# An adaptive-layernorm attention block: a narrower first part of the scale, and four accumulators copied out early

## The chip, the cores and the metric

The kernel runs on one core of a Trainium2 chip. The core has a matrix engine (TensorE, "PE" in the profile), a vector engine (VectorE, "DVE"), an activation engine (ScalarE, "ACT"), GpSimd ("POOL"), and a queue engine (SyncE, "SP") that issues most transfers from HBM. Each engine runs its own instructions in order and waits on semaphores for the others. The metric is device time in microseconds (us) of one execution; lower is better.

## The reference

The inputs are x [2, 256, 1152], a conditioning vector c [2, 1152], and the bf16 weights wqkv [1152, 3456], wo [1152, 1152] and w_mod [1152, 6912].

```python
mod = (silu(c) @ w_mod).reshape(B, 6, 1, D)
shift_a, scale_a, gate_a, ... = [mod[:, i] for i in range(6)]
h = layernorm(x) * (1 + scale_a) + shift_a
q, k, v = split(h @ wqkv, 3)
p = softmax((q @ k.T) * D ** -0.5)
out = x + gate_a * ((p @ v) @ wo)
```

Only the first three sixths of w_mod matter: shift, scale and gate.

## The kernel before

D = 1152 is nine blocks of 128 (`KT`), and the 512 tokens are four tiles of 128 (`TT`), two to a batch. Everything up to the scores is kept transposed: the channel lies on the partitions, the token on the free axis.

**The problem at the start.** h needs scale and shift, each a product of silu(c) with 1152 x 1152 weights, and the projections need h. To have TensorE at work before the shift's weights (`wH`) have come, the kernel uses that h @ w = (xn * (1 + scale)) @ w + shift @ w. `xnT` is the transposed normalized x; `hTs` = `xnT` times (1 + scale), without the shift. The first seven column blocks of q (`NB` = 7, their weights are `wA`) are accumulated from `hTs`: six in `accs[0..5]` (banks of the pool `psum`, 128 x 512 f32 each), the seventh in `acc_last` (`last_acc`). Their shift part is 63 narrow matmuls (`bias_mms`) into `bias_ps`, added when the accumulators are evacuated to `qkT` (`acc_evac`). The other eleven column blocks of q and k, and v, use the full `hT` = `xnT` * (1 + scale) + shift (`modulated`), once the shift is there.

**The scale comes in two column parts.** `KA` = 5: `scale_block(psSA, ...)` gives the scale of channel blocks 0 to 4 from the first 640 columns of `wS`, in nine steps of contraction (kk) of five matmuls each; `psSB` gives blocks 5 to 8 from the other 512. The ones matmul that opens `psSA` makes it 1 + scale. So the accumulation can run with blocks 0 to 4 while the rest of `wS` is on its way.

**The transposes.** `transposes(t, h, ...)` makes half h of tile t: blocks 0 to 4 or 5 to 8 (`HALF` follows `KA`), by TensorE into a bank `tp`; `xnT_copy` brings it to SBUF, on VectorE (`True`) or ScalarE (`False`). Tiles 0 and 1 (batch 0) come before the accumulation; tiles 3 and 2 between its steps.

**The accumulation.** `qkv_half(k, b)` is channel block k for the tokens of batch b: six matmuls of 256 columns, one for each accumulator. `qkv_step(k)` does both batches at once, six of 512. Before: half steps for blocks 0 to 4 of both batches, steps for blocks 5 to 8. `shift_block(kk)` is a step of the shift, nine matmuls from `wH` into `bankH`. After the ninth, VectorE copies the shift to `sh_bf` and `sh`.

**What sets the order.** `pin()` fixes the order of PE, DVE, ACT and SP as written in the source; all recorded operations therefore have line L76 in the profile, and are told apart by their tiles. The pool `psum` has six banks, `psum_pre` two. A transfer of SP waits for the landing of the one eight before it. The load order on SP is x, the first part of `wS` (five transfers), `wA` rows 0 to 4 (three), the rest of `wS` (two), `wA` rows 5 to 8 (two), `wH` (five), then the other wqkv columns (`wq_t`), the gate's weights and wo.

**After the shift** come 18 `modulated` pieces, each one channel block of one batch; every third on ScalarE, the others on VectorE. Before, both evacuations of accumulator 1 stand after the fifteenth piece. Then VectorE forms the gate (`gacc`, 18 operations), TensorE the eleven `ps` blocks, the scores, v, p @ v and the last product.

Of the kernel before, what the change touches and what calls it, by code (L numbers as in the profile page):

```python
# [10 lines left out]
F32 = mybir.dt.float32  # L11
# [5 lines left out]
def kernel(  # L17
# [10 lines left out]
    P = 128  # L28
    B, N, D = x.shape
    T = B * N  # L30
    KT = D // P
# [7 lines left out]
    NACC = 6  # L39
    NB = 7  # L40
    WA = NB * P
    KA = 5
    CA = KA * P
    NRS = 96
    NRH = 54
    KH = KA
    N_JUNK = 11

    x_f = x.rearrange("b n d -> (b n) d")
# [4 lines left out]
    const = ctx.enter_context(tc.tile_pool(name="const", bufs=1))  # L54
    wpool = ctx.enter_context(tc.tile_pool(name="wpool", bufs=1))
    act = ctx.enter_context(tc.tile_pool(name="act", bufs=1))
# [3 lines left out]
    psum_pre = ctx.enter_context(tc.tile_pool(name="psum_pre", bufs=2, space=PSUM))  # L60
# [22 lines left out]
    vec = _Rec(nc.vector, dve_seq)  # L83
    sca = _Rec(nc.scalar, act_seq)
    ten = _Rec(nc.tensor, pe_seq)

    def pin(seq):
# [11 lines left out]
        out=ident, in_=ident, compare_op=ALU.not_equal, fill=1.0, base=0,  # L99
# [49 lines left out]
    def load_mod(tile_, which, k0, k1, c0, c1):  # L149
        spq.dma_start(out=tile_[:, k0:k1, c0:c1], in_=wmod_v[:, k0:k1, which, c0:c1])  # L150

    def load_wA(k0, k1):
        spq.dma_start(out=wA[:, k0:k1, :], in_=wqkv_v[:, k0:k1, 0:WA])
# [4 lines left out]
    load_wA(1, 3)  # L158
    load_wA(3, KA)
    load_mod(wS, 1, 0, 5, CA, D)  # L160
    load_mod(wS, 1, 5, KT, CA, D)
    load_wA(KA, 7)
    load_wA(7, KT)
    for k0, k1 in ((0, 2), (2, 4), (4, 6), (6, 8), (8, 9)):
        load_mod(wH, 0, k0, k1, 0, D)

# [5 lines left out]
    def fillers(n):  # L172
# [10 lines left out]
        out=scT_f.rearrange("p k b -> p b k"),  # L183
# [7 lines left out]
    def sc_rhs(kk, n):  # L191
        return scT_rep[:, kk].rearrange("p r b -> p (r b)")[:, 0:n]
# [9 lines left out]
    def dve_stats(t, s):  # L202
        vec.bn_stats(out=stats[t][:, s, :], in_=x_sb[:, t, s * CW : (s + 1) * CW])
# [6 lines left out]
    def dve_norm(t):  # L210
        vec.scalar_tensor_tensor(
            out=nb[:, t : t + 1], in0=mv_all[:, t, 0:1], scalar=-1.0, in1=rstd[:, t : t + 1],
            op0=ALU.mult, op1=ALU.mult,
        )
        vec.tensor_scalar(
            out=xn[:, t, :], in0=x_sb[:, t, :], scalar1=rstd[:, t : t + 1], scalar2=nb[:, t : t + 1],
            op0=ALU.mult, op1=ALU.add,
        )
# [15 lines left out]
    def act_norm(t):  # L234
        sca.activation(out=xn[:, t, :], in_=x_sb[:, t, :], func=ACT.Identity,
                       bias=nb[:, t : t + 1], scale=rstd[:, t : t + 1])

    tps = {}
    HALF = ((0, KA), (KA, KT))

    def transposes(t, h, pool, tag):
        k0, k1 = HALF[h]
        tp = pool.tile([P, KH, P], BF16, tag=tag, name="tp")
        for k in range(k0, k1):
            ten.transpose(tp[:, k - k0, :], xn[:, t, k * P : (k + 1) * P], ident)
        tps[t, h] = tp

    def xnT_copy(t, h, on_dve):
        k0, k1 = HALF[h]
        dst, srct = xnT[:, k0:k1, t * P : (t + 1) * P], tps[t, h][:, : k1 - k0, :]  # L250
        if on_dve:
            vec.tensor_copy(out=dst, in_=srct)
        else:
            sca.copy(out=dst, in_=srct)


    s1p = const.tile([P, KT, B], F32)
# [3 lines left out]

    psSA = psum_pre.tile([P, KA, NRS], F32, tag="pre")
    ten.matmul(psSA.rearrange("p j r -> p (j r)"), lhsT=ones_bf[0:1, :],
# [3 lines left out]
    def scale_block(ps_, n, k0, k1, kk, ones=True):  # L267
        for j in range(k0, k1):
            ten.matmul(
                ps_[:, j - k0, :], lhsT=wS[:, kk, j * P : (j + 1) * P], rhs=sc_rhs(kk, n),  # L270
                start=(kk == 0 and j == k0 and not ones), stop=(kk == KT - 1), skip_group_check=True,
            )

    def scaled(k, b, scalar):
        sl = slice(b * N, (b + 1) * N)
        vec.tensor_scalar(out=hTs[:, k, sl], in0=xnT[:, k, sl], scalar1=scalar, scalar2=None, op0=ALU.mult)

    def qkv_half(k, b):
        sl = slice(b * N, (b + 1) * N)
        for f in range(NACC):  # L280
            ten.matmul(
                accs[f][:, sl], lhsT=wA[:, k, f * P : (f + 1) * P], rhs=hTs[:, k, sl],
                start=(k == 0 and b == 0), stop=False, skip_group_check=True,
            )

    def qkv_step(k):
        for f in range(NACC):
            ten.matmul(
                accs[f], lhsT=wA[:, k, f * P : (f + 1) * P], rhs=hTs[:, k, :],
                start=False, stop=(k == KT - 1), skip_group_check=True,  # L290
            )

    def last_acc(k0, k1):
        for k in range(k0, k1):
            ten.matmul(
                accs[NACC], lhsT=wA[:, k, NACC * P : NB * P], rhs=hTs[:, k, :],
                start=(k == 0), stop=(k == KT - 1),
            )

    def shift_block(kk):  # L300
        for j in range(KT):
            ten.matmul(
                psH[:, j, :], lhsT=wH[:, kk, j * P : (j + 1) * P], rhs=sc_rhs(kk, NRH),
                start=(kk == 0 and j == 0), stop=(kk == KT - 1), skip_group_check=True,
            )
# [17 lines left out]
    xnT_copy(1, 1, False)  # L323
    scale_block(psSA, NRS, 0, KA, 2)
    scale_block(psSA, NRS, 0, KA, 3)
    dve_stats(2, 1)
    transposes(0, 0, psum, "mm")
    transposes(0, 1, psum, "mm")
    xnT_copy(0, 0, True)
    dve_stats(2, 2)  # L330
    dve_aggr(2)
    act_norm(3)
    xnT_copy(0, 1, False)
    for kk in range(4, KT):
        scale_block(psSA, NRS, 0, KA, kk)
    transposes(3, 0, psum_pre, "pre")
    xnT_copy(3, 0, False)

    accs = []
    for f in range(NACC):  # L340
# [2 lines left out]

    scaled(0, 0, psSA[:, 0, 0:1])
    vec.tensor_copy(out=s1p[:, 0:KA, :], in_=psSA[:, :, 0:B])
    for k in range(1, 4):
        scaled(k, 0, s1p[:, k, 0:1])
    dve_norm(2)
    scaled(4, 0, s1p[:, 4, 0:1])
    qkv_half(0, 0)  # L350
    qkv_half(1, 0)
    qkv_half(2, 0)
    transposes(2, 0, psum_pre, "pre")
    xnT_copy(2, 0, True)
    qkv_half(3, 0)
    transposes(3, 1, psum_pre, "pre")
    xnT_copy(3, 1, False)
    qkv_half(4, 0)
    transposes(2, 1, psum_pre, "pre")
    xnT_copy(2, 1, False)  # L360
    for k in range(KA):
        scaled(k, 1, s1p[:, k, 1:2])
    for k in range(3):
        qkv_half(k, 1)
    psSB = psum_pre.tile([P, KT - KA, NRH], F32, tag="pre")
    for kk in range(KT):
        scale_block(psSB, NRH, KA, KT, kk, ones=False)
# [2 lines left out]
        for b in range(B):  # L370
            scaled(k, b, s1p[:, k, b : b + 1])
    qkv_half(3, 1)
    qkv_half(4, 1)


    bankH = psum_pre.tile([P, 512], F32, tag="pre")
    psH = bankH[:, 0 : KT * NRH].rearrange("p (k r) -> p k r", k=KT)
    bias_ps = bankH[:, KT * NRH : KT * NRH + NB * B].rearrange("p (f b) -> p f b", b=B)
    accs.append(psum_pre.tile([P, T], F32, tag="pre", name="acc_last"))
    qkv_step(5)  # L380
    qkv_step(6)
    shift_block(0)
    shift_block(1)
    qkv_step(7)
    for kk in range(2, 5):
        shift_block(kk)
    last_acc(0, 3)
    shift_block(5)
    shift_block(6)
    shift_block(7)  # L390
    qkv_step(8)
    acc0_sb = const.tile([P, T], F32)
    sca.copy(out=acc0_sb, in_=accs[0])
    last_acc(3, 6)
    shift_block(8)
    vec.tensor_copy(out=sh_bf, in_=psH[:, :, 0:B])
# [16 lines left out]
    def modulated(i):  # L413
        k, b = divmod(i, B)
        sl = slice(b * N, (b + 1) * N)
        if i % 3 == 2:
            sca.activation(
                out=hT[:, k, sl], in_=xnT[:, k, sl], func=ACT.Identity,
                bias=sh[:, k, b : b + 1], scale=s1p[:, k, b : b + 1],
            )  # L420
        else:
            vec.tensor_scalar(
                out=hT[:, k, sl], in0=xnT[:, k, sl],
                scalar1=s1p[:, k, b : b + 1], scalar2=sh[:, k, b : b + 1],
                op0=ALU.mult, op1=ALU.add,
            )
# [3 lines left out]
    def acc_evac(f, b, on_dve):  # L430
        sl = slice(b * N, (b + 1) * N)
        if on_dve:
            vec.tensor_scalar(
                out=qkT[:, f, sl], in0=accs[f][:, sl], scalar1=bias_sb[:, f, b : b + 1],
                scalar2=None, op0=ALU.add)
        else:
            sca.activation(
                out=qkT[:, f, sl], in_=accs[f][:, sl], func=ACT.Identity,
                bias=bias_sb[:, f, b : b + 1], scale=1.0)

    for i in range(15):
        modulated(i)
    vec.tensor_copy(out=bias_sb, in_=bias_ps)
    for b in range(B):
        acc_evac(1, b, True)
    for i in range(15, KT * B):
        modulated(i)
    accs[0] = acc0_sb
    for f, on_dve in ((2, False), (3, True), (4, False), (5, True), (6, False), (0, True)):
        for b in range(B):  # L450
            acc_evac(f, b, on_dve)

# [35 lines left out]
    for b in range(B):  # L488
        vec.tensor_scalar(
            out=gacc[:, b, :], in0=wg_k[0], scalar1=scT_f[:, 0, b : b + 1], scalar2=None, op0=ALU.mult  # L490
        )
        for kt in range(1, KT):
            vec.scalar_tensor_tensor(
                out=gacc[:, b, :], in0=wg_k[kt],
# [37 lines left out]
    for b in range(B):  # L532
# [7 lines left out]
        for i in range(NQ):  # L540
            sca.activation(
                out=p_f[:, i, :], in_=s_ps[:, i, :], func=ACT.Exp,
# [43 lines left out]
    for t in range(TT):  # L586
        b = t // NQ
# [67 lines left out]
```

## Time and profile before

| | |
|---|---|
| median of 3 runs | 103.08 us (102.88 to 103.28) |
| the profiled execution, time | 102.94 us |
| the profiled execution, span from first to last instruction | 101.2 us |
| mean granted TensorE clock | 0.994 |
| busy: PE, DVE, ACT, POOL | 94.1, 71.7, 30.9, 29.1 us |
| HBM read, written | 19.76 MB, 1.18 MB |

The span is what the profile's clock starts and ends with; the rest of the time (1.7 us) lies around it. "Busy" of PE counts matmuls whose ends are modelled, so it overstates how full the engine is; starts of matmuls are what can be compared. In a timeline line the numbers are start and length, then engine, line, operation, out<-in, engine array, shapes and count; the bracket at its end gives the idle time before it and what ended that. In the chain a line has start, length, and the engine or transfer. In a windows line the columns are the stretch and its length, then busy time and instruction count of PE, PEld, DVE, ACT and POOL, the granted clock, the share of the DMA engines, and GB/s.

### The profile page before, as it was taken

The page shows a single profiled execution, that of the slowest core. Times are in us where ns is not written, and L with a number is a line of the kernel's source. Part 1 is how long each engine was busy: PE and PEld are TensorE (multiplying, and loading weights), DVE is VectorE, ACT ScalarE, POOL GpSimd, SP SyncE. Part 2 cuts the span into 40 slices and gives each one's busy share as a digit, 9 for nine tenths or more (in the row PEclk, how much of TensorE's full clock was granted, in tenths as well). Part 3 has the DMA queues.
Part 4 walks back from the last instruction along what each step waited for, and adds up shares of the span by engine and source line. Part 5 has one row for each costly group of instructions (what it writes and reads, how often), then busy time and mean ns, then how long its engine had stood idle before and what let it go on. Part 6 is the DMA issues. An engine that isn't in the chain of part 4 may idle for free.

```text
span 101.2 us, 1878 instructions
## 1 busy us (share of the span) xinstructions
PE 94.1 (93%) x769; PEld 58.1 (57%) x773; DVE 71.7 (71%) x129; ACT 30.9 (31%) x61; POOL 29.1 (29%) x29
## 2 busy tenths in 40 slices
PE   1999899999999799999999999999998999999970
PEld 0228779956657244444447865656567765665650
DVE  1599754240029999999999999955626857989960
ACT  5378904000039932422422013146215500000000
POOL 5038300000000000000799100000898000999700
PEclk9999999999999999999999999999999999999997
DMA  2999999999999999999999700000000000303122
GB/s 38 371 319 343 392 357 367 384 391 385 349 369 342 373 383 333 302 323 327 331 379 389 284 13 0 0 0 0 6 0 3 0 0 0 117 6 117 69 80 85
DMA packets 16963, 21.06 MB, mean 208 GB/s; under 512 B 827, under 2 KB 12603, under 8 KB 16955
## 3 DMA queue, kind: packets, MB, share of 16 engines
q1 hardware_dynamic: 16523, 20.34, 59.6%
q10 hardware_dynamic: 432, 0.61, 2.2%
q8 instruction: 6, 0.10, 0.4%
q14 instruction: 2, 0.02, 0.1%
HBM read 19.76 MB, written 1.18 MB: 207 GB/s over the span
## 4 chain that ended last, share of the span: by engine, by line
PE 66%; DMA 18%; SPq 7%; DVE 5%; issue 1%; ACT 0%
PE ps L76 59%; DMA wH<-in_w_mod_dram 12%; SPq L76 7%; DMA wS<-in_w_mod_dram 7%; PE s_ps L76 4%; DVE hT L76 3%; PE acc_t L76 1%; DVE qkT L76 1%; PE bankH L76 1%; PE acc_last L76 1%; DVE pT L76 0%; PE pT_ps L76 0%; ACT o_sb L76 0%; DVE sh_bf L76 0%; DVE sh L76 0%
## 5 line engine op out<-in xcount | busy, mean ns | idle before, releaser
L497 POOL PARTITION_ALL_REDUCE gate_bc<-gacc x2 | 14.1, 7067 | 51.7 <-DVE gacc L76 36.5
L76 DVE SCALAR_TENSOR_TENSOR gacc<-wG,scT_f,gacc 128x1152 f32<-128x1152 bf16 x16 | 27.4, 1714 | 0.6
L76 PE MATMUL ps<-hT,wq_t 128*128 128x512 bf16 x97 | 21.6, 379 | 0.6 <-DVE hT L76 0.5
L76 PE MATMUL ps<-wq_t,hT 128*128 128x384 bf16 x108 | 17.7, 326 | 0.0
L76 PEld LDWEIGHTS <-wq_t 128*128 128x128 bf16 x99 | 9.5, 98 | 12.3 <-DVE hT L76 1.2
L76 PE MATMUL ps<-wO,attnT 128*128 128x384 bf16 x99 | 16.2, 326 | 0.0
L76 PEld LDWEIGHTS <-attnT 128*128 128x128 bf16 x117 | 10.9, 98 | 6.7
L76 PEld LDWEIGHTS <-hT 128*128 128x128 bf16 x108 | 10.6, 98 | 6.9
L76 PE MATMUL acc_t<-hTs,wA 128*128 128x256 bf16 (+1 forms) x83 | 13.0, 302 | 0.3
L76 PEld LDWEIGHTS <-wA 128*128 128x128 bf16 x156 | 10.2, 97 | 4.1 <-DMA wA<-in_wqkv_dram 0.4
L571 POOL TENSOR_TENSOR wo_last<-wO,gate_bc 128x384 bf16<-128x384 bf16 x9 | 9.8, 1125 | 7.8 <-issue 7.8
L76 ACT CAST qkT<-ps 128x512 bf16<-128x512 f32 x11 | 6.5, 587 | 13.0 <-PE ps L76 13.0
L76 DVE TENSOR_TENSOR o_sb<-ga,x_sb 128x384 bf16<-128x384 f32 x11 | 7.9, 722 | 0.4
L76 DVE TENSOR_TENSOR ga<-ps,gate_bc 128x384 f32<-128x384 f32 x11 | 6.1, 554 | 2.7 <-PE ps L76 2.6
L76 ACT CAST v_sb<-ps 128x384 bf16<-128x384 f32 x8 | 3.7, 482 | 11.8 <-PE ps L76 11.8
L76 DVE CAST sh_bf<-bankH 128x18 bf16<-128x18 f32 x1 | 0.2, 177 | 8.3 <-PE bankH L76 8.3
L76 ACT CAST o_sb<-ps 128x64 bf16<-128x64 f32 x1 | 0.2, 213 | 17.4 <-PE ps L76 17.4
L76 DVE BATCH_NORM_STATS2 stats<-x_sb 128x6 f32<-128x384 bf16 x9 | 4.6, 543 | 0.9 <-DMA x_sb<-in_x_dram 0.9
L76 PE MATMUL junk_ps<-junk_rhs,ident 128*128 128x512 bf16 x11 | 5.1, 628 | 0.0
L76 ACT COPY xnT<-tp 128x512 bf16<-128x512 bf16 (+1 forms) x6 | 3.6, 619 | 3.5 <-PE tp L76 3.5
L76 PE MATMUL ps<-pT,v_sb 128*128 128x256 bf16 x36 | 4.1, 272 | 0.3 <-DVE pT L76 0.3
L76 DVE CAST attnT<-ps 128x512 bf16<-128x512 f32 (+1 forms) x6 | 3.5, 602 | 1.1 <-PE ps L76 1.1
(77 smaller groups left out, 86.5 us busy)
## 6 DMA issues: line engine op xcount, KB each, us to landing
wq_t<-in_wqkv_dram SPq DMA_DIRECT2D x5, 864.0 KB, 10.8
wG<-in_w_mod_dram SPq DMA_DIRECT2D x3, 864.0 KB, 10.7
wO<-in_wo_dram SPq DMA_DIRECT2D x3, 864.0 KB, 9.7
wH<-in_w_mod_dram SPq DMA_DIRECT2D x4, 576.0 KB, 11.0
wA<-in_wqkv_dram SPq DMA_DIRECT2D x4, 448.0 KB, 7.4
wS<-in_w_mod_dram SPq DMA_DIRECT2D x4, 320.0 KB, 6.2
wq_t<-in_wqkv_dram SPq DMA_DIRECT2D x3, 288.0 KB, 10.3
out_dram<-o_sb SPq DMA_DIRECT2D x3, 288.0 KB, 2.1
```

Of the source, the lines that this page charges most:

```text
L76: r = fn(*a, **k)
L497: ar = nc.gpsimd.partition_all_reduce(gate_bc[:, b, :], gacc[:, b, :], P, bass.bass_isa.ReduceOp.add)
L571: nc.gpsimd.tensor_tensor(out=wo_last[:, k, :], in0=wo_k[k][:, D - TAILW :], in1=gate_bc[:, B - 1, D - TAILW :], op=ALU.mult)
```

## The change

- `KA` goes from 5 to 4: the scale's first column part has four blocks (512 columns), the second five (640). The transposes' halves become four and five blocks, and `KH`, the size of `tp`, becomes `KT - KA`. Block 4 of the accumulation is no longer done in halves but as a `qkv_step`, behind `psSB`. `wA` is loaded in rows 0, 1-2, 3, and after the rest of `wS` rows 4-5 and 6-8.
- The copies of tiles 0 and 1 are all on ScalarE, in a row, ahead of `act_norm(3)`; the statistics of tile 2 follow in one piece on VectorE. The first half of tile 3 is transposed after three half steps instead of ahead of all of them. The second half of tile 2 is transposed after the half steps of batch 1, just before `psSB`; its copy moves to VectorE.
- `qkv_step(8)` moves ahead of shift steps 6 and 7, and `last_acc(0, 3)` ahead of step 4. After `qkv_step(8)`, four accumulators are copied to SBUF in f32 (`acc_sb`): 0 and 2 by ScalarE, 1 and 3 by VectorE. Before, ScalarE copied accumulator 0 alone.
- All 18 `modulated` pieces come first, then `bias_sb`, then every evacuation: 4, 5, 6 from PSUM, 0 to 3 from SBUF.

```diff
-    KA = 5
+    KA = 4
-    KH = KA
+    KH = KT - KA
...
-    load_wA(KA, 7)
-    load_wA(7, KT)
+    load_wA(KA, 6)
+    load_wA(6, KT)
...
-    dve_stats(2, 1)
     transposes(0, 0, psum, "mm")
     transposes(0, 1, psum, "mm")
-    xnT_copy(0, 0, True)
+    xnT_copy(0, 0, False)
+    xnT_copy(0, 1, False)
+    dve_stats(2, 1)
     dve_stats(2, 2)
     dve_aggr(2)
     act_norm(3)
-    xnT_copy(0, 1, False)
     for kk in range(4, KT):
         scale_block(psSA, NRS, 0, KA, kk)
-    transposes(3, 0, psum_pre, "pre")
-    xnT_copy(3, 0, False)
...
     dve_norm(2)
-    scaled(4, 0, s1p[:, 4, 0:1])
     qkv_half(0, 0)
     qkv_half(1, 0)
     qkv_half(2, 0)
+    transposes(3, 0, psum_pre, "pre")
+    xnT_copy(3, 0, False)
     transposes(2, 0, psum_pre, "pre")
     xnT_copy(2, 0, True)
     qkv_half(3, 0)
     transposes(3, 1, psum_pre, "pre")
     xnT_copy(3, 1, False)
-    qkv_half(4, 0)
-    transposes(2, 1, psum_pre, "pre")
-    xnT_copy(2, 1, False)
     for k in range(KA):
         scaled(k, 1, s1p[:, k, 1:2])
     for k in range(3):
         qkv_half(k, 1)
+    transposes(2, 1, psum_pre, "pre")
+    xnT_copy(2, 1, True)
...
     qkv_half(3, 1)
-    qkv_half(4, 1)
...
+    qkv_step(4)
     qkv_step(5)
     qkv_step(6)
     shift_block(0)
     shift_block(1)
     qkv_step(7)
-    for kk in range(2, 5):
-        shift_block(kk)
+    shift_block(2)
+    shift_block(3)
     last_acc(0, 3)
+    shift_block(4)
     shift_block(5)
+    qkv_step(8)
+    acc_sb = act.tile([P, 4, T], F32, tag="a1")
+    for f in range(4):
+        if f % 2 == 0:
+            sca.copy(out=acc_sb[:, f, :], in_=accs[f])
+        else:
+            vec.tensor_copy(out=acc_sb[:, f, :], in_=accs[f])
     shift_block(6)
     shift_block(7)
-    qkv_step(8)
-    acc0_sb = const.tile([P, T], F32)
-    sca.copy(out=acc0_sb, in_=accs[0])
     last_acc(3, 6)
     shift_block(8)
...
-    for i in range(15):
+    for i in range(KT * B):
         modulated(i)
     vec.tensor_copy(out=bias_sb, in_=bias_ps)
-    for b in range(B):
-        acc_evac(1, b, True)
-    for i in range(15, KT * B):
-        modulated(i)
-    accs[0] = acc0_sb
-    for f, on_dve in ((2, False), (3, True), (4, False), (5, True), (6, False), (0, True)):
+    for f in range(4):
+        accs[f] = acc_sb[:, f, :]
+    for f, on_dve in ((4, False), (5, True), (6, False), (0, True), (1, True), (2, False), (3, True)):
         for b in range(B):
             acc_evac(f, b, on_dve)
```

More of the change, by code (lines that the diff above doesn't have):

```diff
@@ L345 @@
     vec.tensor_copy(out=s1p[:, 0:KA, :], in_=psSA[:, :, 0:B])
-    for k in range(1, 4):
+    for k in range(1, KA):
         scaled(k, 0, s1p[:, k, 0:1])
     dve_norm(2)
-    scaled(4, 0, s1p[:, 4, 0:1])
     qkv_half(0, 0)
```

## The prediction

> **What bounds the kernel now.** I read the chain that ended last first, then TensorE's and VectorE's timelines between 10 and 36 us, then the busy table and the windows for the transfers. TensorE is busy 93% of the span, so a change pays only where it removes a hole in TensorE's stream or work from it. The chain in order of time shows the two places that the diff touches:
>
> ```profile
> 14.64 12.10 DMA wH<-in_w_mod_dram
> ...
> 26.79 0.63 PE bankH L76 x18
> 27.41 1.29 PE acc_t L76 x6
> 28.71 0.65 PE acc_last L76 x3
> 29.36 0.24 PE bankH L76 x9
> ...
> 29.92 2.65 DVE hT L76 x10
> 32.57 0.09 DVE bias_sb L76
> ...
> 32.68 0.88 DVE qkT L76 x2
> 33.56 0.26 DVE hT L76
> ```
>
> The path runs through the shift weights wH until 26.74, through TensorE's last shift and accumulator work until 29.60, and then through VectorE: ten `hT` pieces, `bias_sb`, two evacuations of accumulator 1, and only then the `hT` piece that TensorE lacks. From 33.87 the chain is TensorE to the end, but for 0.44 us of `pT` and the tail. TensorE's timeline shows the holes:
>
> ```profile
> 10.81 0.81 PE L76 MATMUL psSA<-scT_rep,wS 128*128 128x96 bf16 x15 [0.22 <-DMA wS<-in_w_mod_dram]
> ...
> 12.08 2.44 PE L76 MATMUL acc_t<-hTs,wA 128*128 128x256 bf16 x18
> 14.36 0.44 PE L76 MATMUL tp<-ident,xn 128*128 128x128 bf16 x5
> ...
> 18.36 1.07 PE L76 MATMUL psSB<-scT_rep,wS 128*128 128x54 bf16 x36
> 19.27 4.06 PE L76 MATMUL acc_t<-hTs,wA 128*128 128x256 bf16 x23
> ...
> 26.79 0.63 PE L76 MATMUL bankH<-scT_rep,wH 128*128 128x54 bf16 x18 [0.16 <-DMA wH<-in_w_mod_dram]
> ...
> 33.87 20.07 PE L76 MATMUL ps<-hT,wq_t 128*128 128x512 bf16 x90 [0.54 <-DVE hT L76]
> ```
>
> Matmul ends are modelled, so I count holes between starts. The `ps` matmuls follow each other every 215 ns from 31.66; the eighth was due at 33.16 and started at 33.87, and the second block started at 34.35 where 33.59 was due: this hole is 0.76 us. Between shift blocks 5 and 6 the step is 0.343 instead of 0.025 us: 0.32 us of waiting for wH. The rate of the transfers comes from the windows, one of 2304-byte rows (wH) and one of 768-byte rows (the v part of wqkv):
>
> ```profile
> 21.00:27.00 6.00, 5.78 (x80) 3.48 (x81) 0.32 (x2) 0.00 (x0) 0.00 (x0) 1.00 1.06 377
> 45.00:52.00 7.00, 6.95 (x33) 3.16 (x33) 6.89 (x5) 1.76 (x3) 3.34 (x1) 1.00 1.10 337
> ```
>
> The last column is GB/s: narrower rows move somewhat slower, with the engines full in both.
>
> **The change, part by part.**
>
> *The hole in `hT`.* VectorE now does its twelve `hT` pieces in one run, ScalarE its six, and all evacuations follow. In the trace VectorE starts a piece every 0.256 us and needs 0.34 for one; ScalarE every 0.49 and 0.585. Counted from `sh_bf` (29.62), VectorE starts 0.30 later and ends its twelfth at 0.30 + 11 x 0.256 + 0.34 = 3.46; ScalarE starts at 0.36 and ends its sixth at 0.36 + 5 x 0.49 + 0.585 = 3.40. TensorE wants the last pair at 33.376 - 29.62 = 3.76, the pair before at 3.54 and gets it at 3.20. All 0.76 us go. Next in line is a PSUM bank for the second and later blocks: blocks 7 to 10 take banks 0 to 3, freed by the new copies; block 11 takes accumulator 4, which ScalarE evacuates by about 34, and is wanted after 37.
>
> *The four copies.* They are added work: on ScalarE two of 0.59 (the old copy of accumulator 0), on VectorE two with no row. The bf16 copy of 512 (`pT`, 0.425) and the f32 cast of 512 (`attnT`, 0.691) bound one; I take 0.65, as its source is f32. They wait for TensorE's step 8, and behind VectorE's pair stands `sh_bf`, behind ScalarE's the first `hT`. Counted from the start of step 8, its fourth matmul is through at 1.0 and VectorE's second copy at about 1.9; the shift ends 1.34 (shift 6 and 7 0.46, `last_acc` 0.65, shift 8 0.23) after step 8's 1.29, at 2.6, and `sh_bf` would start at 2.85. So the copies cost nothing on the path while those three steps cover them, and up to 0.65 without. Both engines stand idle there in the trace (8.3 and 10.5 us), and an evacuation that reads `acc_sb` takes 0.341 where one that reads `acc_t` takes 0.474. The page "VectorE: DVE Perf Modes" of the Trainium skill (Rules for kernel authors) advises a copy from PSUM to SBUF ahead of an operation only when many follow; here one follows each half, so by the rule the three added copies are a loss of some 1.9 us of engine time, and if that stood on the path the sum would end above 103.08.
>
> *The front: earlier start.* The first wS part shrinks from 1440 to 1152 KB in as many rows (1152, now of 1024 bytes). Everything up to wA's row 2 lands earlier by e. If a row costs the same whatever its width, e is 0; by bytes at the 331 GB/s of 5 to 10 us it is 0.89. Between: 768 bytes at 337 GB/s are 2.28 ns, 2304 at 377 are 6.11, so 2.5 ps a byte; 256 bytes x 1152 rows x 2.5 ps = 0.74. I take e = 0.7, nearest this row. The Trainium skill's "DMA: Bandwidth & Descriptors" (Why small descriptors are slow) gives a fixed overhead of about 3 beats of 32 bytes a packet: 35 beats then stand against 43, e as an estimate would be 0.19 of some 4.3 us, 0.8, and the sum 0.1 better.
>
> In before, TensorE began the accumulators at 12.08 (0.34 after the first `hTs`), waited 0.30 for wA's rows 1 and 2 (issued at 6.40, 6.6 us to landing), and was through three halves at 14.36. Both causes move by e, so this becomes 14.36 - e. What must keep up: ScalarE now copies all four early transposes (0.59 and 0.69 each, against 0.492 on VectorE); the third can start at 9.95, when its transposes are through, and is done at about 10.55. VectorE, rid of its copy, is free at 10.65 (11.21 before); the first `hTs` is due at 11.7 - e = 11.0. `act_norm(3)` slips from 11.5 to about 12.4, wanted at 13.6. POOL's `rstd` of tile 2 comes earlier with its statistics.
>
> *The front: added work on TensorE behind that point.* Transposes: 18 (4+4+5+5) in place of 13, 56 ns each, +0.28. `psSB`: 45 matmuls in place of 36, 25 ns each, +0.23. Fourth block: 6 x 216 ns in place of 12 x 109, 0. The second batch's first `hTs` now waits for both copies of tokens 2 and 3, 0.26 after the transposes, 0.42 (VectorE; ScalarE's 0.59 ends alike) and 0.29: about +0.12. A new wait before step 4: from the last `psSB` matmul, `s1p` starts 0.22 later and two `hTs` end 0.91 later, with the semaphore 0.96; before, two halves (1.31) covered it, now one (0.66) and the issue step: +0.27. Sum 0.90. The bounds of the two waits are 0 and 0.6 together.
>
> *The end of the shift.* Step 8 moves ahead of shift 6, so the 0.32 hole is filled: wH's last rows are due at 27.6 and TensorE comes to them later. TensorE reaches shift 6 then without waiting, and the shift ends at +0.90 - 0.32 - e = -0.12.
>
> *Queues.* SP issues as many transfers in the same order; each waits for the landing eight before, so the early ones go out up to e sooner, and the bytes up to wH are the same. Its later waits for wS and wH to be free come with `psSB` and shift 8, within 1 us of before.
>
> *Sum.* -0.12 - 0.76 = -0.88 us: span 101.2 to 100.3. The profiled execution took 102.94, 0.14 under the median of 103.08; against the median 102.2.
>
> *Is the rest still TensorE's?* `gacc` starts some 0.6 earlier (29.8 + twelve `hT` + eight evacuations at 0.39 and 0.26 = 35.5, before 36.08), TensorE 0.88 earlier, so VectorE loses 0.3 of its lead. The second exponential frees its bank at 70.17 and TensorE wants it at 57.71 + 9 x 1.464 = 70.9: 0.7 becomes 0.4. POOL's `wo_last` ends at 95.55 and is wanted from 96.3 on, its ninth block a microsecond later. Nothing turns up.
>
> **Rivals.** (a) *The front gives back what the tail gains.* If a row costs the same whatever its width, e = 0 and the shift ends 0.58 later: -0.18, 102.9. For it: engines full in every window; against: the two rates above. With both waits at the upper bound and e = 0.4 it is -0.4. (b) *The hole opens elsewhere*, at a v bank or where ScalarE is late with evacuations: gain 0.2 to 0.5, 102.7. Against: the margins of 0.4 and 3 us. (c) *Slower: step 4 waits for its weights.* wA's rows 4 and 5 now stand behind a second wS part of 1440 KB. The like piece landed at 19.45 (issued 9.65, 9.8 to landing) with 224 KB more before it, 0.6 at 377 GB/s, so I expect 18.9; wanted at 19.5. From 20.4 on all gain is gone; from 20.9 it is slower by half a per cent; landing at 21.0, 1.5 late, gives 102.2 + 1.5 = 103.7. Against: from 18.9 there are 1.5 us to the deciding point. (d) *Better*: no waits in the middle and e = 0.9: 0.51 - 0.32 - 0.9 - 0.76 = -1.5, 101.6.
>
> **How the numbers follow.** Forecast 0.64 (own range 101.9 to 102.55), (a) 0.16, (b) 0.07, (c) 0.07, (d) 0.06. The range runs from halfway to (d) to just past (a): 101.7 to 103.0; it leaves out (c) and the far ends of (d) and (a), about 0.15. Half a per cent (0.52 us) is about what a measurement here can tell from no change: faster is under 102.56. Forecast, (d) and a little of (b) give 0.73; most of (a) and (b) 0.19; slower 0.08.
>
> **What the profile after would show.** Right: no idle before a `ps<-hT` matmul at 31 to 35 us; `ps` blocks in one run of 215 ns steps; first `acc_t` at about 11.3; no wait for wH; a hole of about 0.3 before the first 512-wide `acc_t`; `sh_bf` at about 29.5; `gacc` near 35.5. Wrong: first `acc_t` still near 12 (e is 0), wait for wA before step 4, `sh_bf` started by VectorE's own copy rather than by `bankH`, or a bank wait in the v blocks.

## The result, and the profile after

The changed kernel takes 102.38 us (median of 15 runs, 102.05 to 102.63) against 103.08 for the kernel before (15 runs beside it): ratio 0.994, 95% interval 0.992 to 0.996, so 0.4 to 0.8 us faster. The profiled execution took 102.05, with a span of 100.3, against 102.94 and 101.2. The two profiled executions thus differ by 0.89 and the medians by 0.70; the medians are what counts. The profiled execution of the changed kernel happens to be the fastest of its 15, and what varies between executions is looked into below.

The chain of the kernel after in order of time, start and length:

```profile
6.18 6.10 DMA wA<-in_wqkv_dram
...
18.74 0.18 DVE s1p L76
...
18.95 0.49 DVE hTs L76 x2
...
26.83 1.29 PE acc_t L76 x6
28.12 0.46 PE bankH L76 x18
28.58 0.65 PE acc_last L76 x3
29.22 0.23 PE bankH L76 x9
29.45 0.65 PE acc_last L76 x3
30.10 1.56 PE bankH L76 x63
31.66 21.39 PE ps L76 x99
```

The transfer of wH and VectorE's run from `hT` to `qkT` and back are gone from the chain. From 19.48 on it is TensorE without a break, but for `pT` and the tail. Instead a short way through VectorE, `s1p` and two `hTs`, now stands in the middle. TensorE's timeline after:

```profile
9.91 1.01 PE L76 MATMUL psSA<-scT_rep,wS 128*128 128x96 bf16 x20
11.38 2.43 PE L76 MATMUL acc_t<-hTs,wA 128*128 128x256 bf16 x18 [0.46 <-DVE hTs L76]
13.65 0.61 PE L76 MATMUL tp<-ident,xn 128*128 128x128 bf16 x8
...
17.41 1.30 PE L76 MATMUL psSB<-scT_rep,wS 128*128 128x54 bf16 x45
18.54 4.98 PE L76 MATMUL acc_t<-hTs,wA 128*128 128x256 bf16 x24
23.36 0.61 PE L76 MATMUL bankH<-scT_rep,wH 128*128 128x54 bf16 x18
...
27.96 0.62 PE L76 MATMUL bankH<-scT_rep,wH 128*128 128x54 bf16 x18
...
31.52 21.53 PE L76 MATMUL ps<-hT,wq_t 128*128 128x512 bf16 x99
```

All 99 `ps` matmuls are one run with steps of 0.215 us. The accumulators start 0.70 earlier (11.38 against 12.08), but `ps` only 0.14 earlier (31.52 against 31.66): between the two the lead is used up. VectorE after, around the shift:

```profile
27.30 1.29 DVE L76 COPY acc_sb<-acc_t 128x512 f32<-128x512 f32 x2 [6.30 <-PE acc_t L76]
29.49 0.18 DVE L76 CAST sh_bf<-bankH 128x18 bf16<-128x18 f32 x1 [0.90 <-PE bankH L76]
...
29.78 3.16 DVE L76 TENSOR_SCALAR hT<-xnT,s1p,sh 128x256 bf16<-128x256 bf16 x12
32.87 0.16 DVE L76 COPY bias_sb<-bankH 128x14 f32<-128x14 f32 x1
```

Its two copies end 0.90 before TensorE releases `sh_bf`; the twelve `hT` pieces follow in one run.

### The profile page after: what moved, and what is told of

The parts are those of the page before. It is cut to its first block, busy times and chain, and to the rows that moved or that the text cites. A ratio compares the mean times of both kernels' runs of the same rounds, so it can differ in the third digit from the quotient of the medians.

```text
span 100.3 us, 1871 instructions
## 1 busy us (share of the span) xinstructions
PE 92.7 (92%) x767; PEld 57.0 (57%) x767; DVE 72.3 (72%) x131; ACT 31.5 (31%) x62; POOL 29.0 (29%) x29
## 4 chain that ended last, share of the span: by engine, by line
PE 83%; DMA 11%; DVE 1%; SPq 1%; issue 0%; ACT 0%
PE ps L76 61%; PE acc_t L76 11%; DMA wA<-in_wqkv_dram 6%; DMA x_sb<-in_x_dram 5%; PE s_ps L76 4%; PE bankH L76 4%; PE acc_last L76 2%; PE psSB L76 1%; PE tp L76 1%; SPq L76 1%; DVE hTs L76 0%; DVE pT L76 0%; PE pT_ps L76 0%; ACT o_sb L76 0%; DVE s1p L76 0%
## 5 line engine op out<-in xcount | busy, mean ns | idle before, releaser
L76 PEld LDWEIGHTS <-wA 128*128 128x128 bf16 x150 | 9.6, 96 | 5.2 <-DMA wA<-in_wqkv_dram 0.8
L76 ACT CAST v_sb<-ps 128x384 bf16<-128x384 f32 x8 | 3.7, 480 | 11.6 <-PE ps L76 11.6
L76 DVE COPY acc_sb<-acc_t 128x512 f32<-128x512 f32 x2 | 1.3, 685 | 6.3 <-PE acc_t L76 6.3
L76 ACT COPY acc_sb<-acc_t 128x512 f32<-128x512 f32 x2 | 1.1, 588 | 11.2 <-PE acc_t L76 11.2
## 6 DMA issues: line engine op xcount, KB each, us to landing
wq_t<-in_wqkv_dram SPq DMA_DIRECT2D x5, 864.0 KB, 10.7
wG<-in_w_mod_dram SPq DMA_DIRECT2D x3, 864.0 KB, 10.7
wH<-in_w_mod_dram SPq DMA_DIRECT2D x4, 576.0 KB, 11.7
wq_t<-in_wqkv_dram SPq DMA_DIRECT2D x3, 288.0 KB, 10.8
```

Of the source, the lines that this page charges most:

```text
L76: r = fn(*a, **k)
```

## The experiments

The theory (A) was the prediction's sum: the end of the change gives 0.76 at `hT` and 0.32 at wH, the front costs 0.90 of added work and waits less the earlier landing. The rival (B): the front's earlier start is the gain. Each time below has its ratio to the kernel before, run beside it.

| kernel | median us | ratio (95%) |
|---|---|---|
| before, beside each of three groups of these | 103.09, 103.10, 103.22 | |
| tail_only | 102.20 | 0.990 (0.987 to 0.994) |
| old_front, and again | 102.06, 102.05 | 0.990 (0.987 to 0.993), 0.990 (0.986 to 0.993) |
| front_only | 103.45 | 1.004 (1.001 to 1.007) |
| order_no_copies | 103.08 | 1.0005 (0.997 to 1.004) |
| changed kernel, two more times | 102.22, 102.49 | 0.994 (0.991 to 0.998), 0.992 (0.989 to 0.995) |
| step8_back | 102.48 | 0.996 (0.993 to 0.998) |
| two_halves | 102.09 | 0.994 (0.991 to 0.996) |
| front_fix, and again | 102.13, 102.45 | 0.992 (0.988 to 0.995), 0.993 (0.989 to 0.996) |

**The end alone: tail_only.** The kernel before, with

```diff
     qkv_step(8)
-    acc0_sb = const.tile([P, T], F32)
-    sca.copy(out=acc0_sb, in_=accs[0])
+    acc_sb = act.tile([P, 4, T], F32, tag="a1")
+    for f in range(4):
+        if f % 2 == 0:
+            sca.copy(out=acc_sb[:, f, :], in_=accs[f])
+        else:
+            vec.tensor_copy(out=acc_sb[:, f, :], in_=accs[f])
...
-    for i in range(15):
+    for i in range(KT * B):
         modulated(i)
...
```

and the evacuations in the order of the change:

> The kernel before with only the end of the change: the four accumulator copies (behind step 8, which stays where it was, after shift 7) and all modulated pieces ahead of the evacuations. Theory A (three terms: the hT hole gives 0.76, the wH hole 0.32, the new front costs 0.90 less what the earlier landing gives): 0.76 us faster than before, 102.3, ratio 0.993; ps matmuls in one run of 215 ns steps; VectorE's second copy ends before shift 8 does, so sh_bf still starts near 29.6. Theory B (the earlier start of the front is what made the change faster, and the hole at hT merely moves): within 0.1 us of before, ratio 0.999.

0.9 us faster (0.7 to 1.4): A holds, B falls. The `ps` matmuls are again one run, and VectorE's second copy still ends 0.45 before `sh_bf`, although step 8 stands after shift 7 here:

```profile
28.00 1.29 DVE L76 COPY acc_sb<-acc_t 128x512 f32<-128x512 f32 x2 [6.23 <-PE acc_t L76]
29.73 0.18 DVE L76 CAST sh_bf<-bankH 128x18 bf16<-128x18 f32 x1 [0.45 <-PE bankH L76]
```

**The copies: order_no_copies.** The kernel before, with only the order of the evacuations:

```diff
-    for i in range(15):
+    for i in range(KT * B):
         modulated(i)
     vec.tensor_copy(out=bias_sb, in_=bias_ps)
-    for b in range(B):
-        acc_evac(1, b, True)
-    for i in range(15, KT * B):
-        modulated(i)
     accs[0] = acc0_sb
-    for f, on_dve in ((2, False), (3, True), (4, False), (5, True), (6, False), (0, True)):
+    for f, on_dve in ((1, True), (2, False), (3, True), (4, False), (5, True), (6, False), (0, True)):
```

> The kernel before with all 18 modulated pieces first and every evacuation after them, but without the three added copies: accumulators 1 to 3 stay in their banks. Theory A (the copies are needed as they free the banks): the first ps block runs through, the second waits for VectorE's two evacuations of accumulator 1, which end near 34.0 where the block is due at 33.6: 0.3 us faster than before, ratio 0.997. Rival (the order alone does it): 0.76 us faster, ratio 0.993.

No change in time that the runs show (one of the twelve took 546.58 us; the ratio leaves it out, and without it the median is 102.90): the interval goes from 0.3 us faster to 0.4 slower, so the rival's 0.76 falls, and the expected 0.3 lies at its edge. The trace says why so little is left: the hole moves from inside the first block to the front of the second, which waits for its bank. (The bracket names ScalarE's evacuation, where the expectation had VectorE's of accumulator 1; the two end at 34.21 and 34.24.)

```profile
31.82 2.10 PE L76 MATMUL ps<-hT,wq_t 128*128 128x512 bf16 x9
34.26 2.10 PE L76 MATMUL ps<-hT,wq_t 128*128 128x512 bf16 x9 [0.33 <-ACT qkT L76]
```

Counted between starts it is 0.50 us instead of 0.76 (the expected gain of 0.3 would leave 0.46). The order is worth its gain only with the copies that free the banks.

**The front: front_only and old_front.** front_only is the changed kernel with the shift order, the one copy and the evacuations of before; against the changed kernel:

```diff
-    qkv_step(8)
...
     shift_block(6)
     shift_block(7)
+    qkv_step(8)
+    acc0_sb = const.tile([P, T], F32)
+    sca.copy(out=acc0_sb, in_=accs[0])
...
-    for i in range(KT * B):
+    for i in range(15):
         modulated(i)
...
```

old_front is the changed kernel with the transposes, copies, half steps and loads of before; against the changed kernel:

```diff
-    KA = 4
+    KA = 5
-    KH = KT - KA
+    KH = KA
...
-    xnT_copy(0, 0, False)
-    xnT_copy(0, 1, False)
-    dve_stats(2, 1)
+    xnT_copy(0, 0, True)
...
+    qkv_half(4, 1)
...
-    qkv_step(4)
...
```

> The changed kernel's front (KA 4) with the end of before: step 8 after shift 7, one copy, two evacuations among the modulated pieces. Theory A: TensorE starts the accumulators about 0.7 earlier and reaches shift 6 about 0.2 later than before, which is when wH lands (26.7); so within 0.2 us of before, ratio 1.000 to 1.002, with the hole at hT as before. Theory B: 0.4 to 0.7 us faster, ratio 0.993 to 0.996.

> The changed kernel with the front of before: KA is 5 again, with the transposes, copies and half steps in their old places; step 8 ahead of shift 6, the copies and the late evacuations as in the change. Theory A: 0.76 + 0.32 = 1.08 us faster than before, 102.0, ratio 0.9895, so faster than the changed kernel by 0.2 to 0.4; shift ends 0.3 earlier than before. Theory B: the gain of the front is missing, 0.1 to 0.4 us faster than before, ratio 0.996 to 0.999.

The front alone makes the kernel slower by 0.4 us (0.1 to 0.7), a little more than A had; B is refuted from this side too. With the old front and the new end the kernel takes 102.06, 1.0 us less than before (expected 1.08). front_only's profile shows where the lead ends:

```profile
26.56 0.39 PE L76 MATMUL bankH<-scT_rep,wH 128*128 128x54 bf16 x9
27.19 0.63 PE L76 MATMUL bankH<-scT_rep,wH 128*128 128x54 bf16 x18 [0.24 <-DMA wH<-in_w_mod_dram]
...
34.27 1.94 PE L76 MATMUL ps<-hT,wq_t 128*128 128x512 bf16 x8 [0.55 <-DVE hT L76]
```

It waits for wH twice, 0.2 us ahead of shift block 4 and 0.4 ahead of shift block 6, counted between starts. wH's rows 6 and 7 land at 27.14; in four of the five profiles with the old front they land at 26.4 to 26.7, in one at 27.7, and in the eight with the new front at 26.7 to 28.3.

**What holds wH: step8_back.** The changed kernel with step 8 and the copies after shift 7:

```diff
-    qkv_step(8)
...
     shift_block(6)
     shift_block(7)
+    qkv_step(8)
...
```

> The changed kernel with step 8 back behind shift blocks 6 and 7, the four copies after it. By the prediction's term for the wH hole: TensorE then waits 0 to 0.4 us for wH ahead of shift block 6, so 0 to 0.4 slower than the changed kernel, ratio to before 0.995 to 0.998. Rival (VectorE's second copy of about 0.65 ends after shift 8 and holds sh_bf back): sh_bf is released by nothing of TensorE, and the loss is more than the hole before shift block 6.

The profile has the hole, larger than expected: 0.46 by the timeline, 0.62 between starts.

```profile
26.26 0.61 PE L76 MATMUL bankH<-scT_rep,wH 128*128 128x54 bf16 x18
27.33 0.63 PE L76 MATMUL bankH<-scT_rep,wH 128*128 128x54 bf16 x18 [0.46 <-DMA wH<-in_w_mod_dram]
```

In time the kernel is 0.26 above the changed one beside it (102.48, 102.22), which the intervals don't separate. With the old front, moving step 8 gained nothing that shows (tail_only 102.20, old_front 102.06): tail_only's profile has no wait for wH at all, as TensorE began the shift at 23.61 there and at 23.16 in the kernel before, while rows 6 and 7 landed at 26.41 and 26.74. So the 0.32 of the prediction is a term that is there in some executions only. The rival on `sh_bf` falls: it is released by TensorE, 0.45 after the copies.

**The waits in the middle of the front: two_halves, front_fix.**

two_halves, against the changed kernel:

```diff
-    for k in range(3):
+    for k in range(2):
         qkv_half(k, 1)
...
+    qkv_half(2, 1)
     qkv_half(3, 1)
```

front_fix has both lines of that, and:

```diff
     xnT_copy(3, 1, False)
+    transposes(2, 1, psum_pre, "pre")
     for k in range(KA):
         scaled(k, 1, s1p[:, k, 1:2])
+    xnT_copy(2, 1, True)
     for k in range(2):
         qkv_half(k, 1)
-    transposes(2, 1, psum_pre, "pre")
-    xnT_copy(2, 1, True)
```

> The changed kernel with the third half step of batch 1 moved behind psSB, so that two half steps (1.31 us) cover the way from psSB over s1p to the first hTs of the second part. Theory F, in which that uncovered way (0.28 in the profile) is part of the front's cost: the hole before the first 512-wide acc_t goes, 0.25 us faster than the changed kernel, ratio to before 0.991. Rival (what TensorE gains there it loses to transfers, wA's rows 4 and 5 or wH): a wait for wA before step 4 or for wH before shift 6 takes its place, no change.

> As two_halves, and the second half of tile 2 is transposed directly after tile 3's, where TensorE waits 0.14 for the first hTs of batch 1; its copy on VectorE follows those hTs. Theory F: another 0.14 us of TensorE's stream, 0.25 to 0.4 us faster than the changed kernel, 102.0, ratio to before 0.988 to 0.990, with a possible wait of 0.2 for wA's rows 4 and 5, which landed at 18.8 and 19.3 and are then wanted at 19.1. Rival: as for two_halves, no change.

> The changed kernel with both waits in the middle of its front filled, again, beside the other two. The first profile had shift block 0 at 22.9 (23.3 in the changed kernel) and a span of 99.8 (100.2 and 100.3). If that is the usual case, 0.3 to 0.4 us faster than the changed kernel beside it, ratio to before 0.988 to 0.991; if not, within 0.15.

In two_halves the hole before the first 512-wide `acc_t` is gone, but in its profiled execution x landed a microsecond late, so nothing can be read from where the shift begins; the time is not told apart from the changed kernel's. In the first profile of front_fix the shift begins 0.4 earlier than in the changed kernel and the span is 99.8. The second looks otherwise: its step 4 waits 0.38, counted between starts, for wA's rows 4 and 5, which land at 19.39, and its time is that of the changed kernel beside it (102.45, 102.49). Over both groups of runs the gain is about 0.15 us and not established. The rival of late transfers is seen at work, though not every time.

**The same kernels again: after_again, after_3, old_front_2.**

> The changed kernel once more, with a second profile, beside the three that follow. Ratio to before 0.991 to 0.996. Theory F (the new front costs what it gains: matmul starts show the shift reached at about the same time as with the old front, and the first wS part of narrower rows moves fewer bytes in the first 10 us): about 2480 to 2500 KB moved by 10 us again, against 2590 to 2630 in the four profiles with the old front; the last wS piece of the first part lands near 10.4; shift block 0 starts at 23.3 to 23.4. Rival (the first profile of the changed kernel was lucky in its front, and the front is a gain of 0.3 or more): shift block 0 starts below 23.2.

> The changed kernel, as the measure for the two beside it: ratio to before 0.992 to 0.996; shift block 0 at 23.3.

> The old front with the new end, again, now beside the changed kernel and front_fix on one chip, with a second profile. Theory F (front of the change about even, within 0.2 us): within 0.2 us of the changed kernel beside it. Theory A of the prediction (front costs 0.2 net): 0.2 faster than the changed kernel. In the profile about 2600 KB moved by 10 us and the first accumulator matmul at 12.1 to 12.5, against 2500 and 11.3 to 11.4 with the new front; no wait for wH.

after_again came out as theory F expected: 2510 KB by 10 us, the last wS piece at 10.35, shift block 0 at 23.30. after_3 did not: shift block 0 starts at 24.64 instead of 23.3. old_front_2 has 2620 KB, its first accumulator matmul at 12.13 and no wait for wH.

Taken together, the changed kernel has a median of 102.39 (35 runs) and the old front with the new end 102.07 (16 runs): the front costs 0.3 us net (95% by resampling these runs: 0.1 to 0.6). In the last group the pair stands at 102.49 and 102.05, twice what theory F allowed. So A's sign stands, as it does in front_only; that the cost is more than F's 0.2 is not shown.

Where executions differ can be read from the profiles. From the start of shift block 0 to the end of the span it is 78.0 us before, and 76.9 in each of the nine profiles with the new end (tail_only among them), with either front; only step8_back, with its wait for wH, has 77.5. The 1.1 between is the prediction's 0.76 and 0.32. So with the new end nothing behind that point varied but that wait, and the front decides through one number, the start of shift block 0. In after_3, old_front and old_front_2 (the changed kernel's 23.36 stands further up):

```profile
24.64 0.61 PE L76 MATMUL bankH<-scT_rep,wH 128*128 128x54 bf16 x18
24.22 0.61 PE L76 MATMUL bankH<-scT_rep,wH 128*128 128x54 bf16 x18
22.90 0.61 PE L76 MATMUL bankH<-scT_rep,wH 128*128 128x54 bf16 x18
```

The five profiles with the old front have it at 22.90 to 24.22, the five with the changed front at 23.30 to 24.64, and the middle ones (23.61 and 23.36) even stand the other way round from the times. One profile of each kernel can't show what the 0.3 us is made of, and it stays open. after_3 shows one way in which the new front loses. Its profiled execution took 103.34; the accumulators began 0.71 later than in the first profile, and TensorE waits in the middle of `psSB` for the second part of wS:

```profile
17.89 0.44 PE L76 MATMUL tp<-ident,xn 128*128 128x128 bf16 x5
18.17 0.79 PE L76 MATMUL psSB<-scT_rep,wS 128*128 128x54 bf16 x25
19.30 0.68 PE L76 MATMUL psSB<-scT_rep,wS 128*128 128x54 bf16 x20 [0.35 <-DMA wS<-in_w_mod_dram]
```

Its transfers were slow early on. The windows view of 5 to 10 us, last column GB/s, in the kernel before:

```profile
5.00:10.00 5.00, 4.88 (x45) 2.77 (x45) 4.77 (x14) 3.99 (x7) 2.92 (x7) 1.00 1.00 331
```

The same window in the changed kernel's first profile:

```profile
5.00:10.00 5.00, 3.88 (x44) 2.35 (x44) 4.85 (x14) 4.16 (x8) 2.69 (x7) 1.00 0.96 303
```

And in after_3:

```profile
5.00:10.00 5.00, 4.89 (x42) 2.37 (x40) 4.85 (x13) 3.91 (x8) 2.81 (x7) 1.00 0.97 271
```

All profiles together: 311 to 331 GB/s in the five with 640 columns, 271 to 309 in the eight with 512. The narrower part is smaller and comes sooner, but by 10 us some 100 KB less have moved. That an old-front execution with late transfers waits less can be seen in one case: the first profile of old_front (102.92), with wH's rows 6 and 7 at 27.7, has no wait for wA, wH or the second part of wS. It isn't a clean comparison: TensorE itself was late there, with the accumulators from 13.45 (last section), 1.32 later than in old_front_2, which is all of the difference between the two profiles.

## Why the prediction was right, and where not

- **The hole in `hT`, 0.76:** right. It is gone in every kernel with the new end, VectorE and ScalarE end as reckoned (3.46 and 3.36 after `sh_bf` starts), and the end alone is worth 0.9 us (0.7 to 1.4). That the copies are needed for it is shown by order_no_copies.
- **The copies cost nothing:** right. VectorE's takes 0.685 (0.65 taken), the cover is 0.90 (0.9 reckoned), and 0.45 remains even with step 8 in its old place.
- **e = 0.7:** the first accumulator matmul came 0.70 earlier in the first pair of profiles. Over all of them the last wS piece of the first part lands at 10.8 to 11.6 with the old front and at 10.35 to 10.7 with the new (11.2 in after_3), so about 0.9 between the middle ones: nearer to the bound by bytes (0.89) than to e = 0. What the prediction didn't have is that less has moved behind it: by 10 us some 100 KB less, and wH's rows 6 and 7 land at 27.15 in the middle one of eight profiles, at 26.53 in that of five with the old front.
- **Added work, 0.90:** right. From the end of the third half step to step 5 it took 6.22 before and 7.13 after, 0.91 more; the wait before step 4 is 0.28 (0.27 reckoned), that of batch 1 0.14 (0.12).
- **The wH hole, 0.32:** gone after, as said. It was in the one profile of before; tail_only and order_no_copies, with the same front, reach the shift 0.5 later and have none. The step took a wait that one execution showed for a lasting one.
- **The sum:** -0.88 for a measured -0.70 (-0.4 to -0.8). For the profiled executions it is right term by term (span 100.3, time 0.89 less), and that is in part luck: the changed kernel's was the fastest of its 15 runs, and after_3's took 103.34. In the medians, the end with step 8 moved gives 1.02 for 1.08 (old_front), and the front costs about 0.3 for 0.2 (changed kernel against old_front; front_only 0.4). So the front is the term that was mis-sized most, though 0.3 and 0.2 are not told apart by these runs. What makes up the cost is not shown. It is not wH in the changed kernel: none of its three profiles waits for it once step 8 stands ahead. The late landings seen with the new front are the second part of wS (0.5, after_3), wA's rows 4 and 5 (0.1 in step8_back, 0.4 in the second front_fix) and, with step 8 in its old place, wH (0.6 in all in front_only, 0.6 in step8_back). How often each of these waits occurs was not measured; one profile per run can't tell.
- **Rivals (a) and (c):** the condition of (a), e = 0, did not occur. Nor did (c) in the three profiles of the changed kernel: wA's rows 4 and 5 landed at 18.83 (18.9 reckoned), 19.28 and 20.41, each time before step 4. The waits just listed are of (c)'s kind, for other transfers too, and at 0.1 to 0.6 us, not the 1.5 that would have decided.
- **Rivals (b) and (d):** (b) did not occur: the v blocks run without a wait (one run of 108 matmuls from 56.81), and `gacc` starts at 35.43 (35.5 reckoned). (d) did not occur.

Of the versions run, old_front has the lowest median: 102.06, ratio 0.990. tail_only, two_halves and front_fix (its first group) lie within 0.15 of it and are not told apart.

## What to carry to other kernels

Work that waits for a late scalar should stand in one run on its engines, ahead of anything that only frees banks; if the banks are wanted in the meantime, free them by copies while the engines idle. An order that starts TensorE earlier by making the first load smaller needs the rest to be fed earlier too, and here it gained nothing: count the matmuls and the waits that the split adds (0.90 us against an earlier start of 0.70), and what lands just in time. A forecast from one profiled execution against another can be exact and still miss the median, when a term of it (a wait of 0.3 us for a transfer) comes and goes between executions.

## What the runs showed of the hardware that was not expected

With rows of 1024 instead of 1280 bytes, in the same number, the core's transfers moved some 20 GB/s less (5 to 10 us: 318 and 298 on the mean of five and eight profiles). The order of the loads behind them differs too, and no run changes the row alone, so that the rows are the cause is likely and not shown.

In the first profile of old_front, 128-column transposes followed each other every 107 ns until 11.7 us and every 56 later, where the other executions are at 56 from 8.1 to 8.8 us on; the start of the accumulation slipped to 13.45:

```profile
9.05 1.16 PE L76 MATMUL tp<-ident,xn 128*128 128x128 bf16 x9
10.01 1.01 PE L76 MATMUL psSA<-scT_rep,wS 128*128 128x96 bf16 x10
10.81 1.12 PE L76 MATMUL tp<-ident,xn 128*128 128x128 bf16 x9
11.77 1.23 PE L76 MATMUL psSA<-scT_rep,wS 128*128 128x96 bf16 x25
```

The windows view prints a granted clock of 1.00 over 7.5 to 11.7 us all the same. But the trace's records of the clock only begin at 11.75 us in this execution, and at 5.1 to 8.6 us in the other twelve, which agrees with the steps of the matmuls in each: where there is no record yet, the view prints 1.00. The Trainium skill's "TensorE: Matmul & The Clock Gate" (Part 1: The HAM clock gate) gives these two steps, 106.7 and 55.6 ns, for a cold and a warm array, and says that the change depends on where a free-running window falls; the steps agree, and the column doesn't show them.

ScalarE evacuates 256 columns of f32 in 0.46 to 0.48 us from PSUM and in 0.52 from SBUF; for VectorE it is the other way round, 0.47 to 0.48 and 0.34 to 0.35.
